# Layerscale on one core: the 4-row head of y loaded as one transfer or as two

## The chip, the core and the metric

The kernel runs on one core of a Trainium2 chip. The metric is device time in microseconds, the median over several runs. The core has a tensor engine (PE), a vector engine (DVE), a scalar engine (ACT), GpSimd (POOL) and a sync engine (SP). SP and ACT issue the transfers of this kernel; each has a queue of its own, and both queues are served by the same 16 transfer engines.

## The reference

```python
B, S, D = 1024, 16, 512          # x, y: bf16 [1024, 16, 512], gamma: bf16 [512]
def reference(x, y, gamma):
    return x + gamma * y
```

Flattened, x, y and the output are 16384 rows of 512 values, 1 KB a row and 16.8 MB a tensor.

## The kernel before

Each of the 128 partitions holds 128 rows. The tensors are cut into three blocks (BLOCKS) of 4, 64 and 60 rows per partition; within a block, partition p holds consecutive rows of memory, so a load of a whole block reads one run of 4, 64 or 60 KB for each partition, and each run is one packet. All of y stays in SBUF (y_sb) and is multiplied, added to and stored in place; x_sb is smaller and is used twice.

The order of all work is written out by hand in lists. SP lists the transfers of the sync engine, ACT those of the scalar engine: ('y', 0, 4) loads rows 0 to 3 of each partition's 128 rows of y, ('x', 4, 68, 4) loads rows 4 to 67 of x to x_sb from place 4 on, ('g',) loads gamma and ('s', 4, 68) stores rows. The function ring walks such a list and emits waits and transfers: L129 loads gamma, L132 x, L135 y, L138 stores. DVE lists the multiplications ('m', piece) and additions ('a', piece) over the five PIECES of 8, 16, 44, 52 and 8 rows; they are L180 and L189. Every wait goes through the helper _take (L35), which waits for a semaphore and sets it back.

Two constants shape the start. EARLY says how many entries of each list are moved to the very front of the program, ahead of its barriers (the loop at the end of the kernel function): two of SP's, one of ACT's. HOLD and AHEAD hold the rest back: before its entry number AHEAD, each of the two queues waits for one step of a semaphore (s_held) that TensorE gives when the load named HOLD has landed. TensorE itself then waits for gamma, spreads it over the partitions by a product with a row of ones (L152), and VectorE casts the result to gamma_sb (L154). VectorE takes a third step of s_held in place of waiting for the HOLD load. need(loads, c) emits the waits for the loads that a piece touches, in the order of the lists. The load named RELEASE, x rows 68 to 119, lets the stores begin (s_go).

So the start before is: SP issues y rows 0 to 3, then y rows 4 to 67; ACT issues x rows 0 to 3; when y rows 0 to 3 have landed, SP issues x rows 4 to 67 and y rows 68 to 127, and ACT issues gamma. The first multiplication covers rows 0 to 7 and thus needs y rows 4 to 67 too.

Of the kernel before, what the change touches and what calls it, by code (L numbers as in the profile page):

```python
# [9 lines left out]


SP = [
    ('y', 0, 4),
    ('y', 4, 68),
    ('x', 4, 68, 4),
    ('y', 68, 128),
# [2 lines left out]
]  # L19
ACT = [('x', 0, 4, 0), ('g',), ('s', 4, 68), ('s', 0, 4), ('s', 68, 128)]  # L20

EARLY = (2, 1)

HOLD, AHEAD = ('y', 0, 4), (2, 1)

RELEASE = ('x', 68, 120, 24)

# [10 lines left out]
def kernel(  # L38
# [74 lines left out]
    def ring(eng, what, n_early, n_ahead):  # L113

        known, went = 0, False
        for k, w in enumerate(what):
            kind = w[0]
            if k == n_ahead:
                _take(s_held[eng], 1, eng)
            need = frees(w) if kind == "x" else pieces_of(w[1], w[2]) + list(w[3:]) if kind == "s" else []  # L120
            need = max((order[c] + 1 for c in need), default=0)
            if kind == "s" and not went:
                _take(s_go, 1, eng)
                went = True
            if need > known:
                eng.wait_ge(s_add, need)
                known = need
            if kind == "g":
                i = eng.dma_start(out=gamma_row, in_=gamma.unsqueeze(0)).then_inc(s_gamma, 16)  # L129
            elif kind == "x":  # L130
                to = x_sb[:, w[3] : w[3] + w[2] - w[1], :]
                i = eng.dma_start(out=to, in_=rows_of(xf, w[1], w[2])).then_inc(s_load[w], 16)  # L132
            elif kind == "y":
                r = slice(w[1], w[2])
                i = eng.dma_start(out=y_sb[:, r, :], in_=rows_of(yf, w[1], w[2])).then_inc(s_load[w], 16)  # L135
            else:
                r = slice(w[1], w[2])
                i = eng.dma_start(out=rows_of(of, w[1], w[2]), in_=y_sb[:, r, :]).then_inc(s_out, 16)  # L138
            if k < n_early:
                early.append(i.ins)  # L140

    ring(nc.sync, SP, EARLY[0], AHEAD[0])
    ring(nc.scalar, ACT, EARLY[1], AHEAD[1])

# [89 lines left out]
```

## Time and profile before

| what | us |
|---|---|
| median of 3 runs (lowest, highest) | 119.66 (119.55, 119.72) |
| span of the profiled execution | 118.2 |
| its own time beyond the span | not recorded; the median is 1.5 longer than the span |
| VectorE busy | 70.1 |
| TensorE busy | 0.6 |
| bytes read, written | 33.56 MB, 16.78 MB |
| first issue by SP, by ACT | 0.00, 0.13 |
| first multiplication starts | 23.95 |
| last addition ends | 94.40 |

The span begins with SP's first transfer instruction and ends with its last wait. In the rows of the profile "DMA" is the busy share of the 16 transfer engines in 40 slices of the span, in tenths, and GB/s what they moved. A DMA issue row (SPq, ACTq) is the time that the issuing engine spent on the instruction, not the transfer. In the view of the DMA queues over a stretch, a packet counts where it starts, so a share can be over 100% when long packets start in a short stretch. The columns there are packets, MB and share of the 16 engines' time. A row of waits is: who waited, for whom, microseconds in total, how often, the longest.

### The profile page before, as it was taken

How to read it: one execution, taken by the hardware profiler on the slowest of the kernel's cores; microseconds unless marked ns; L12 is line 12 of the kernel's file. 1: busy time of each engine (PE TensorE's matmuls, PEld its weight loads, DVE VectorE, ACT ScalarE, POOL GpSimd, SP SyncE). 2: the span in 40 equal slices, each digit the busy share in tenths (PEclk: the TensorE clock that was granted, in tenths of full speed). 3: DMA queues.
4: the chain of work that ended last, by engine and by line, in shares of the span. 5: the costliest groups of instructions: out<-in, count | busy, mean ns of one | idle time of the engine just before them, and what ended most of it. 6: DMA issues, size and time to landing. Idle time of an engine off the chain costs nothing. (4 is left out here: it accounts for less than half of the span.)

```text
span 118.2 us, 91 instructions
## 1 busy us (share of the span) xinstructions
PE 0.6 (0%) x1; PEld 0.1 (0%) x1; DVE 70.1 (59%) x12; POOL 0.2 (0%) x4
## 2 busy tenths in 40 slices
PE   0000100000000000000000000000000000000000
PEld 0000000000000000000000000000000000000000
DVE  0000200089999969999999999999999900000000
POOL 0000000000000000000000000000000000000000
DMA  6999889988899879879969696898899889799793
GB/s 248 461 666 399 355 355 399 665 355 355 355 599 466 355 333 624 374 333 499 499 288 576 288 576 288 360 637 355 355 576 488 355 355 510 333 582 416 333 499 166
DMA packets 1442, 50.33 MB, mean 426 GB/s; under 512 B 161, under 2 KB 162, under 8 KB 546
## 3 DMA queue, kind: packets, MB, share of 16 engines
q1 hardware_dynamic: 864, 33.03, 64.8%
q10 hardware_dynamic: 578, 17.30, 33.9%
HBM read 33.56 MB, written 16.78 MB: 426 GB/s over the span
## 5 line engine op out<-in xcount | busy, mean ns | idle before, releaser
L180 DVE TENSOR_TENSOR y_sb<-y_sb,gamma_sb 128x4096 bf16<-128x4096 bf16 (+3 forms) x5 | 34.7, 6981 | 10.9 <-DVEq L35 10.9
L189 DVE TENSOR_TENSOR y_sb<-x_sb,y_sb 128x4096 bf16<-128x4096 bf16 (+3 forms) x5 | 34.7, 6981 | 1.2 <-DVEq L35 1.1
L154 DVE CAST gamma_sb<-gamma_ps 128x512 bf16<-128x512 f32 x1 | 0.7, 692 | 10.2 <-DVEq L35 10.2
L146 DVE MEMSET ones_row<- 1x128 bf16 x1 | 0.2, 165 | 2.0 <-PEq L51 2.0
L152 PE MATMUL gamma_ps<-gamma_row,ones_row 1*128 1x512 bf16 x1 | 0.6, 581 | 11.6 <-PEq L35 11.6
L152 PEld LDWEIGHTS gamma_ps<-gamma_row,ones_row 1*128 1x128 bf16 x1 | 0.1, 101 | 11.6 <-issue 11.6
L218 POOL MEMSET const-bfloat16-1.0<- 128x1 bf16 x1 | 0.1, 101 | 0.0
L218 POOL MEMSET const-uint8-127<- 128x1 uint8 x1 | 0.1, 101 | 0.0
L218 POOL MEMSET const-float32-0.0<- 128x1 f32 x1 | 0.1, 98 | 0.2 <-issue 0.2
L218 POOL MEMSET const-float32-1.0<- 128x1 f32 x1 | 0.1, 98 | 0.0
## 6 DMA issues: line engine op xcount, KB each, us to landing
y_sb<-in_y_dram SPq DMA_DIRECT2D x1, 7680.0 KB, 57.3
out_dram<-y_sb ACTq DMA_DIRECT2D x1, 7680.0 KB, 23.8
x_sb<-in_x_dram SPq DMA_DIRECT2D x1, 6656.0 KB, 21.7
x_sb<-in_x_dram SPq DMA_DIRECT2D x1, 1024.0 KB, 22.0
y_sb<-in_y_dram SPq DMA_DIRECT2D x1, 512.0 KB, 3.4
x_sb<-in_x_dram ACTq DMA_DIRECT2D x1, 512.0 KB, 4.2
out_dram<-y_sb ACTq DMA_DIRECT2D x1, 512.0 KB, 22.3
y_sb<-in_y_dram SPq DMA_DIRECT2D x1, 23.4
```

The source lines that it names most:

```text
L146: nc.vector.memset(ones_row, 1.0).then_inc(s_ones, 1)
L152: nc.tensor.matmul(gamma_ps, ones_row, gamma_row, start=True, stop=True).then_inc(s_ps, 1)
L154: nc.vector.tensor_copy(out=gamma_sb, in_=gamma_ps).then_inc(s_dve, 1)
L180: nc.vector.tensor_tensor(out=yt, in0=yt, in1=g, op=MULT).then_inc(s_dve, 1)
L189: nc.vector.tensor_tensor(out=yt, in0=xt, in1=yt, op=ADD).then_inc(s_add, 1)
L218: nc = _bacc.Bacc("TRN2", target_bir_lowering=False, num_devices=1)
```

## The change

The first entry of SP's list is replaced by two: rows 0 and 1, then rows 2 and 3. EARLY and AHEAD go from 2 to 3 for SP, so all three first entries stay at the front and ahead of the hold. HOLD names the first of the two, so SP's later entries, gamma and VectorE's step wait for rows 0 and 1; VectorE waits for rows 2 and 3 on their own semaphore. Nothing else differs: the same bytes go to the same places, and ACT's list, VectorE's list and the stores are as before. Within a partition the two halves are runs of 2 KB where the whole was one of 4 KB.

```diff
 SP = [
-    ('y', 0, 4),
+    ('y', 0, 2),
+    ('y', 2, 4),
     ('y', 4, 68),
     ('x', 4, 68, 4),
     ('y', 68, 128),
...
-EARLY = (2, 1)
-
-HOLD, AHEAD = ('y', 0, 4), (2, 1)
+EARLY = (3, 1)
+
+HOLD, AHEAD = ('y', 0, 2), (3, 1)
```

## The prediction

> **What bounds the kernel now.** I read the page first: the 40 slices and the DMA totals.
>
> ```profile
> span 118.2 us, 91 instructions
> DVE  0000200089999969999999999999999900000000
> ...
> DMA  6999889988899879879969696898899889799793
> ...
> DMA packets 1442, 50.33 MB, mean 426 GB/s; under 512 B 161, under 2 KB 162, under 8 KB 546
> ```
>
> VectorE (DVE) is idle in the first fifth and the last fifth, while the transfer engines are at 8 to 9 tenths in nearly every slice. Only the first slice starts empty: its 6 is one microsecond before the first packet. All 50.33 MB pass through 16 engines, and I find no stretch in which they wait for VectorE. So the end is set by two things: when the engines begin, and how long they stay fed.
>
> Next the waits of VectorE, to see what a delay would meet:
>
> ```profile
> DVE y_sb L180 <- DVEq L35: 10.9, 1, 10.9
> DVE gamma_sb L154 <- DVEq L35: 10.2, 1, 10.2
> ...
> DVE y_sb L189 <- DVEq L35: 1.1, 1, 1.1
> ```
>
> Its first multiplication (start 23.95) waits 10.9 us for y's rows 4 to 67 after the gamma cast (12.32 + 0.69); its first addition (43.45) waits 1.1 us for x's rows 4 to 67. VectorE follows the loads. Its last addition ends at 78.17 + 16.23 = 94.40, while the previous stores, on the same queue, still move packets until about 99.3. A delay of the head therefore reaches the end in full: no later hole in the DMA row can swallow it.
>
> Then the issues at the start, from the timeline:
>
> ```profile
> 0.00 0.85 SPq L135 DMA_DIRECT2D y_sb<-in_y_dram  x2
> 0.13 0.38 ACTq L132 DMA_DIRECT2D x_sb<-in_x_dram  x1
> ...
> 3.71 0.33 SPq L132 DMA_DIRECT2D x_sb<-in_x_dram  x1
> 3.90 0.50 ACTq L129 DMA_DIRECT2D gamma_row<-in_gamma_dram  x1
> 4.09 0.43 SPq L135 DMA_DIRECT2D y_sb<-in_y_dram  x1
> ```
>
> The three head loads (y 0 to 3 and y 4 to 67 by SP, x 0 to 3 by ACT) have all been issued by 0.85. When do their packets run? The DMA view of three stretches (0.90 to 2.20, 2.20 to 3.64, 3.64 to 4.00; packets count by their start; q1 is SP's queue, q10 ACT's):
>
> ```profile
> q1 hardware_dynamic: 102, 0.42, 84.8%
> ```
>
> ```profile
> DMA packets 163, 0.60 MB, mean 418 GB/s; under 512 B 16, under 2 KB 16, under 8 KB 163
> q10 hardware_dynamic: 121, 0.50, 85.2%
> q1 hardware_dynamic: 42, 0.11, 18.5%
> ```
>
> ```profile
> q1 hardware_dynamic: 16, 1.05, 689.3%
> q10 hardware_dynamic: 23, 0.03, 21.8%
> ```
>
> This is the heart of it. Until 2.20 there is not one packet of x, though x was issued at 0.13, only 0.13 after y's head, whose first packets run at 1.00. From about 2.2 the two queues alternate. The third load was issued at 0.42, yet until 3.64 no packet of 64 KB starts (all 163 are under 8 KB); then 16 start within 0.36 us, one on each engine. So the loads become ready for the engines one after the other, about 1.2 us apart, and not when they are issued. Now that costs nothing: a head load of 512 KB keeps the engines busy for 8 packets of 0.163 us each, 1.3 us, about as long as the next load takes to become ready.
>
> **The change part by part.**
>
> *Smaller packets.* Rows 0 to 3 are 128 runs of 4 KB; two loads make 256 runs of 2 KB, 16 per engine for 8. A 4 KB packet takes 1.04 x 16 engines x 1.44 us / 147 packets = 0.163 us (stretch 2.20 to 3.64, without the 16 completion writes). A 64 KB packet takes 62.7% x 16 x 4.60 / 19 = 2.43 us (stretch 4.00 to 8.60). The line through both is 0.038 us per KB plus 0.012 per packet. It gives 0.088 for 2 KB, so 8 x (2 x 0.088 - 0.163) = 0.10 us more per engine, with one more completion write 0.11. Bounds: not below 0, since the bytes are the same and the packets more; and 2 KB cannot cost more than two packets of 1 KB, of which gamma's takes 2.9% x 16 x 0.10 = 0.046, so at most 8 x (4 x 0.046 - 0.163) = 0.17, about 0.18 with the completion.
>
> *One more load in the row of loads.* Order of issue after: y 0-1 (SP, 0.00), x 0-3 (ACT, 0.13), y 2-3 (SP, 0.42), y 4-67 (SP, 0.85). Every load has 128 runs, as before. What does a load with 2 KB runs take to become ready? No row shows one. Nearest rows: y's head to x's, 2.21 - 1.00 = 1.21 us as upper end, and 1.05 as lower end, because an engine may have chosen one packet (0.16) ahead; x to y's 64 rows, at most 3.65 - 2.21 = 1.44. If the runs count, the half loads cost the same as the whole one. With 1.21 the four loads are ready at 1.00, 2.21, 3.42 and 4.63, and the 64 KB packets start at 4.63 where they started at 3.65: **+0.98 us**. With 1.05: 4.15, +0.50. With 1.21, 1.44, 1.44: 5.09, +1.44. On the engines: y 0-1 is gone after 8 x 0.088 = 0.7 us, by 1.7 to 2.1 (they start between 1.0 and 1.4), and they idle until x comes; x lasts 1.3 us, until 3.5 to 3.9; y 2-3 follows, done by 4.2 to 4.6, and they idle again until y 4-67. The 0.11 of the smaller packets lies inside this waiting and is not added. The other end is 0: were readiness proportional to bytes, the halves would cost half each, and only the 0.11 would be left. I take +0.98, since issue to first packet hardly follows bytes elsewhere: 1.00 us for 0.5 MB at the start, and 78.7 - 77.4 = 1.3 for a store of 8 MB.
>
> The Trainium skill speaks against this reading. "Perfetto Trace Analysis", section "DMA Instruction — HWDGE (DVE, Sync)", says that the profiled duration of a DMA instruction covers the making of all its descriptors and that the generator is free before that duration ends. By it the third load would be ready by 0.85 and the fourth by 1.27, and the change would cost the packets' 0.11 alone. The trace differs: x's issue ends at 0.51 and its first packet starts after 2.20, so I follow the rows and keep the page's answer as a rival.
>
> *SP's third issue ahead of the barrier.* 0.42 us (0.85 for two). The barrier behind it moves as much; ones_row's MEMSET at 1.99 becomes 2.41. TensorE waits for gamma until 11.56, so this is hidden; without that cover it would cost 0.42.
>
> *The hold.* It now waits for y 0-1. Before, the landing at 3.4 released SP's x load at 3.71. Landings come 0.35 after the last packet, so now about 2.1 + 0.35 = 2.5, and x 4-67, gamma and y 68-127 are issued some 0.9 us earlier. Worth nothing: on SP's queue they stand behind y 4-67, which runs to 23.8; gamma has 10.9 us of slack before L180. Queued behind the held instructions are only these.
>
> *VectorE's added wait* for y 2-3 stands ahead of its wait for y 4-67, which ends some 20 us later: 0.
>
> Sum on the profiled execution: span 118.2 + 0.98 = 119.2. The median of the runs shown, 119.66, has 1.5 us around that span; they stay: 119.66 + 0.98 = 120.64.
>
> **Rivals.**
> (1) *Readiness partly overlaps* (a step of 1.0): 64 KB packets at about 4.0, +0.35: 120.0. For it: one packet of choice ahead on each engine blurs the rows. Against: 16 of 16 engines turned to the third load only after 3.64.
> (2) *Not slower: only packets count.* Place: the engines' choice between queues after 2.2. If y 4-67 was ready early and an engine simply finished x's small packets before turning to 64 KB ones, no load is late and only +0.11 is left: 119.77. It decides if a step is under about 0.9 us, the time that 256 KB (0.7) and the engines' stagger cover. For it: no idle is seen at 3.65, a chance fit if loads are made at a rhythm of their own. Against: y's and x's packets do alternate after 2.2, and x's own lateness is not explained.
> (3) *Faster: the first load becomes ready sooner because it is half as big.* If the 0.63 us between the end of its issue (0.37) and its first packet (1.00) went by bytes, -0.31: 119.35. Against: the 8 MB store above.
> That SP blocks at its third issue would be a fourth; nothing due before 11.56 stands behind it, so it costs nothing by itself.
>
> **Chances.** +0.98 case 0.58; rival 1 0.12; rival 2 0.25; rival 3 0.05. The likeliest case's own range is 120.16 to 121.1; the range reaches down to 119.70 to take in rival 1 and half of rival 2. About 0.2% (0.24 us) is what a measurement can tell: faster is rival 3, 0.05; same is rival 2, 0.25; slower the rest, 0.70.
>
> **What would show it.** In the changed profile no x packet before about 2.2, low DMA share between 1.7 and 2.2 and again near 4.3 to 4.6, and the first 64 KB packets near 4.6; L180 starting at about 24.9. If the 64 KB packets start before 3.9, rival 2 is right. A changed length of the stretch after the head would make all of this wrong.

## The result, and the profile after

The changed kernel takes 120.21 us (median of 5, 120.12 to 120.26) beside 119.69 for the kernel before on the same chip: ratio 1.0043, 95% interval 1.0033 to 1.0054, so +0.52 us. It is slower, as forecast, by about half of the 0.98 that I expected. The profiled execution took 120.16 with a span of 118.8.

The page of the changed kernel:

```profile
span 118.8 us, 93 instructions
...
DMA  5999888998899879979969797898899889798791
...
DMA packets 1586, 50.33 MB, mean 424 GB/s; under 512 B 177, under 2 KB 178, under 8 KB 690
```

There are 144 packets more (128 by the split, 16 completion writes), and the first slice fell from 6 to 5. From the third slice on the row is nearly that of before. The loss is at the very start, and nothing gives it back later. VectorE's waits say the same:

```profile
DVE y_sb L181 <- DVEq L36: 11.3, 1, 11.3
DVE gamma_sb L155 <- DVEq L36: 10.0, 1, 10.0
...
DVE y_sb L190 <- DVEq L36: 1.0, 1, 1.0
```

The line numbers moved by one, the lengths of the waits by 0.4 or less. The first multiplication (L181) starts at 24.60 in place of 23.95, the first addition at 44.05 in place of 43.45: everything moved by about 0.6.

Where the 0.6 arises is read from three stretches of the start. The columns are the stretch, its length, the busy time of the compute engines, the clock, and last the DMA share and GB/s. First the kernel before, then the changed one:

```profile
1.00:2.20 1.20, 0.00 (x0) 0.00 (x0) 0.17 (x1) 0.00 (x0) 1.00 0.92 348
2.20:3.00 0.80, 0.00 (x0) 0.00 (x0) 0.00 (x0) 0.00 (x0) 1.00 1.06 420
3.00:3.40 0.40, 0.00 (x0) 0.00 (x0) 0.00 (x0) 0.00 (x0) 1.00 1.02 420
```

```profile
1.00:2.20 1.20, 0.00 (x0) 0.00 (x0) 0.00 (x0) 0.00 (x0) 1.00 0.80 222
2.20:3.00 0.80, 0.00 (x0) 0.00 (x0) 0.17 (x1) 0.00 (x0) 1.00 1.00 369
3.00:3.40 0.40, 0.00 (x0) 0.00 (x0) 0.00 (x0) 0.00 (x0) 1.00 0.96 389
```

The missing bytes are (348 - 222) x 1.2 + (420 - 369) x 0.8 + (420 - 389) x 0.4 = 151 + 41 + 12 = 204 KB. At 420 GB/s they are 0.49 us, close to the whole result, and three quarters of them are missing before 2.20. (Single traces of the same start differ by about 0.1 us here: the run held on rows 2 and 3 below, which starts like the changed kernel, has 176 GB/s in the first stretch, and the run with a late split, which starts like the kernel before, has 328.) The DMA view of that first stretch shows more, in the changed kernel and then in the kernel before:

```profile
DMA packets 128, 0.27 MB, mean 222 GB/s; under 512 B 7, under 2 KB 7, under 8 KB 128
q1 hardware_dynamic: 119, 0.23, 71.0%
q10 hardware_dynamic: 9, 0.04, 9.3%
```

```profile
DMA packets 102, 0.42 MB, mean 348 GB/s; under 512 B 0, under 2 KB 0, under 8 KB 102
q1 hardware_dynamic: 102, 0.42, 91.9%
```

SP's queue started 112 packets of 2 KB (119 less 7 completion writes) where it had started 102 of 4 KB: half the bytes at almost the same number of packets. At the 0.088 us a packet of the prediction the 16 engines had room for 16 x 1.2 / 0.088 = 218. Yet they were not simply empty: their busy share is 0.80 where it was 0.92, and SP's 71.0% are 71.0% x 16 x 1.2 / 112 = 0.12 us for each packet. The packets of rows 2 and 3, of the same size in the same kernel, take 87.5% x 16 x 0.36 / 60 = 0.084 between 3.64 and 4.00:

```profile
q1 hardware_dynamic: 60, 0.12, 87.5%
```

So part of the loss is emptier engines (0.12 x 1.2 = 0.14 us) and part is packets that last longer; these rows do not show why they do. And x (q10) has already begun: its first packet starts at 1.94 by the trace, while the last packet of rows 0 and 1 starts only at 2.61.

Last, the place at which I expected the second wait, 3.40 to 4.04 and 4.04 to 4.80 in the changed kernel:

```profile
q1 hardware_dynamic: 91, 0.19, 74.6%
q10 hardware_dynamic: 31, 0.07, 26.2%
```

```profile
DMA packets 70, 1.12 MB, mean 1480 GB/s; under 512 B 17, under 2 KB 17, under 8 KB 54
q1 hardware_dynamic: 69, 1.12, 344.9%
```

In the first the shares add up to 100%: rows 2 and 3 (q1) follow x's head (q10) without a hole. In the second, 16 packets of 64 KB start (70 less 54 under 8 KB). The trace has the first at 4.06 and the last at 4.72, where before they started from 3.65 to 3.99; the mean of the 16 is 4.27 for 3.79, 0.48 later. The predicted 4.63 for the first was too late, and the second hole did not come.

### The profile page after: what moved, and what is told of

Read it like the earlier page. It is cut to its first block, busy times and chain, and to the rows that moved or that the text cites. A ratio compares the mean times of both kernels' runs of the same rounds, so it can differ in the third digit from the quotient of the medians.

```text
span 118.8 us, 93 instructions
## 1 busy us (share of the span) xinstructions
PE 0.6 (0%) x1; PEld 0.1 (0%) x1; DVE 70.1 (59%) x12; POOL 0.2 (0%) x4
## 2 busy tenths in 40 slices
DMA packets 1586, 50.33 MB, mean 424 GB/s; under 512 B 177, under 2 KB 178, under 8 KB 690
## 5 line engine op out<-in xcount | busy, mean ns | idle before, releaser
L181 DVE TENSOR_TENSOR y_sb<-y_sb,gamma_sb 128x4096 bf16<-128x4096 bf16 (+3 forms) x5 | 34.6, 6981 | 11.3 <-DVEq L36 11.3
```

Of the source, the lines that this page charges most:

```text
L181: nc.vector.tensor_tensor(out=yt, in0=yt, in1=g, op=MULT).then_inc(s_dve, 1)
```

## The experiments

All times are medians beside the kernel before in the same session. Three theories were put to the test. S, the theory of the prediction: a load's packets become ready (so that an engine can run them) at about 1.0 to 1.2 us per 128 packets, whatever they hold, and short packets cannot cover that time. P: the same, but only the first load is paced so. C: the first 1.2 us of traffic are slow for any load. Beside them K: only the packets' own price counts.

**The short load in third place.**

```diff
 SP = [
     ('y', 0, 4),
-    ('y', 4, 68),
+    ('y', 4, 6),
+    ('y', 6, 68),
...
-EARLY = (2, 1)
+EARLY = (3, 1)
-HOLD, AHEAD = ('y', 0, 4), (2, 1)
+HOLD, AHEAD = ('y', 0, 4), (3, 1)
```

> The 2-row load is moved from first to third place: SP issues y 0 to 3, then y 4 and 5, then y 6 to 67; four loads at the start as in the changed kernel, and about as many packets. Theory P (paced first load: packets of the first load become ready at a fixed pace of about 0.14 us per packet and engine, so short packets waste the engines' time only there, while later loads are made ready behind it): only the packets' price, +0.1 us, about 119.8. Theory S (the recorded one: every load needs its own step of about 1.2 us before its packets can run): +0.5 to +1.0, 120.2 to 120.7. Theory C (the first 1.2 us of traffic are slow, whatever the load): +0.1, as P.

120.20 against 119.78, ratio 1.0033 (1.0021 to 1.0046): +0.4, just under S's range. P and C, which expected +0.1, do not account for it. The stretch 4.20 to 4.50 of this run holds almost only its 2 KB packets:

```profile
4.20:4.50 0.30, 0.00 (x0) 0.00 (x0) 0.00 (x0) 0.00 (x0) 1.00 1.03 328
```

328 GB/s in place of some 420, at a full busy share: these 2 KB packets take about 0.10 us each, not 0.084. The first packet of y 6 to 67 starts at 4.52, the last engine's at 5.25; before, the first 64 KB packets came from 3.65 to 3.99.

Not all of the trace's loss is made there. Its first stretch is slower than that of the kernel before (348 GB/s), though the first load is the same:

```profile
1.00:2.20 1.20, 0.00 (x0) 0.00 (x0) 0.00 (x0) 0.00 (x0) 1.00 0.93 297
```

With 394 for 420 in the next 0.8 us, that is 82 KB or 0.2 us. Whether the kernel or the single execution makes it is not shown.

**A longer load in third place.** The control to it: the third load has 8 rows, in 8 KB packets.

```diff
     ('y', 0, 4),
-    ('y', 4, 68),
+    ('y', 4, 12),
+    ('y', 12, 68),
...
-EARLY = (2, 1)
+EARLY = (3, 1)
-HOLD, AHEAD = ('y', 0, 4), (2, 1)
+HOLD, AHEAD = ('y', 0, 4), (3, 1)
```

> As the run with the short third load, but the third load has 8 rows (8 KB packets, 2.5 us of transfer) in place of 2 rows. S: the third load keeps the engines busy while the fourth is made ready, so the loss of the short third load goes: 0 to +0.1, 119.8 to 119.9. If an additional load at the start costs its step in any case: +0.4, as with the short one, 120.2.

119.81 against 119.72, ratio 1.0006 (0.9998 to 1.0015): nothing that can be told from no change. Its third load runs at nearly full rate until the fourth begins (6.20 by the trace):

```profile
3.80:5.00 1.20, 0.00 (x0) 0.00 (x0) 0.00 (x0) 0.00 (x0) 1.00 1.00 406
5.00:6.10 1.10, 0.00 (x0) 0.00 (x0) 0.00 (x0) 0.00 (x0) 1.00 1.03 424
```

The number of loads ahead of the long one, their place ahead of the barrier and the number of packets are those of the run above. Only the length of the third transfer differs (and with it the length of the fourth), and the 0.4 us goes. So this additional load costs nothing that can be measured, once it lasts long enough.

**The same split where the queue is full.** y's last block in place of its head:

```diff
-    ('y', 68, 128),
+    ('y', 68, 70),
+    ('y', 70, 128),
```

> The same kind of extra load, with 128 packets of 2 KB, is put where the queue is full: y 68 to 127 comes as y 68 and 69 and y 70 to 127, behind x 4 to 67, which keeps the engines busy for some 20 us before. S, in the form that 128 packets need about 1.0 to 1.2 us to become ready: there is time for that, so only the packets' price is left, 0 to +0.1, 119.8 to 119.9. K (the extra packets and the completion cost what the change cost): +0.4 to +0.5, as the changed kernel.

119.80 against 119.72, ratio 1.0005 (0.9996 to 1.0014). Its page counts the very packets of the changed kernel:

```profile
span 118.4 us, 93 instructions
...
DMA packets 1586, 50.33 MB, mean 425 GB/s; under 512 B 177, under 2 KB 178, under 8 KB 690
```

1586 packets, 690 of them under 8 KB, as in the changed kernel, yet without its loss. So the price of the packets and of the completion is at most 0.14% (the interval's end, 0.17 us), and K falls as the cause of the change's 0.52. The late split adds 8 packets per engine, as the change does. Rival 2 of the prediction, in which only the packets are left, falls with it.

**One load with twice the packets.** y's head is one load again, of 256 runs:

```diff
-                i = eng.dma_start(out=y_sb[:, r, :], in_=rows_of(yf, w[1], w[2])).then_inc(s_load[w], 16)
+                to, src = y_sb[:, r, :], rows_of(yf, w[1], w[2])
+                if w[1] == 0:
+                    to = to.rearrange("p (b n) d -> p b n d", b=2)
+                    src = yf[: 4 * P].rearrange("(b p n) d -> p b n d", b=2, p=P)
+                i = eng.dma_start(out=to, in_=src).then_inc(s_load[w], 16)
```

> y's head is one load of 512 KB again, but reads 256 runs of 2 KB in place of 128 of 4 KB (its 512 rows are taken in another order, so that y's head rows meet other rows of x: the output of those rows is another one). P with a pace per packet: the first load takes 16 packets x 0.14 = 2.2 us per engine in place of 1.3, so +0.8 to +0.9, 120.5. C: as the changed kernel, about +0.5, 120.2, since only the first 1.2 us are slow. S: three loads, no further step, +0.1, 119.8.

120.33 against 119.78, ratio 1.0041 (1.0028 to 1.0055). One load of 256 short packets costs what two loads of 128 cost. My reading of S as a step for each load (+0.1) missed, and P's +0.8 to +0.9 was too high; C's +0.5 came. Its stretch of 1.00 to 2.20:

```profile
1.00:2.20 1.20, 0.00 (x0) 0.00 (x0) 0.12 (x1) 0.00 (x0) 1.00 0.84 198
```

198 GB/s, like the changed kernel's 222, with y's head as a single load. So the loss does not need a second load; short packets in the first one are enough. One thing here speaks against loads that become ready strictly one after the other: x's first packet starts at 1.92 in this trace, long before the last of y's 256 (4.73), and the two queues alternate in between.

**A first load of one row.**

```diff
-    ('y', 0, 4),
+    ('y', 0, 1),
+    ('y', 1, 4),
...
-EARLY = (2, 1)
+EARLY = (3, 1)
-HOLD, AHEAD = ('y', 0, 4), (2, 1)
+HOLD, AHEAD = ('y', 0, 1), (3, 1)
```

> The head of y is split 1 and 3 rows in place of 2 and 2: the first load has 1 KB packets and 128 KB. P: the first load still takes about 1.1 us for 8 packets, but moves 128 KB less than the changed kernel's in it, 0.3 us of transfer that comes later: +0.3 against the changed kernel, +0.8 against before, 120.5. S: as the changed kernel, +0.5, 120.2. C, if the slowness is one of bytes per time: +0.5; if it is one of packets per time, as P.

120.60 against 119.78, ratio 1.0060 (1.0047 to 1.0073): +0.7 to +0.8. The expectation of a paced first load (P's +0.8, and C's if it counts packets) holds; S's +0.5, the unchanged loss, missed. The profiled execution took 120.25, the fastest of the five, so its trace shows less than the usual loss. Its DMA view of 1.00 to 2.20:

```profile
DMA packets 149, 0.18 MB, mean 146 GB/s; under 512 B 14, under 2 KB 137, under 8 KB 149
q1 hardware_dynamic: 137, 0.13, 45.0%
```

123 packets of 1 KB (137 less 14 completion writes) where it was 112 of 2 KB and 102 of 4 KB: nearly the same pace, 10 to 12 ns a packet over all engines, with 146, 222 and 348 GB/s. The 102 say the least, since at 0.163 us a packet the engines can run no more than 16 x 1.2 / 0.163 = 118.

**Rows 2 and 3 behind the long load.**

```diff
     ('y', 0, 2),
-    ('y', 2, 4),
     ('y', 4, 68),
+    ('y', 2, 4),
```

(beside the changed kernel).

> The changed kernel with its second and third SP loads exchanged: rows 0 and 1, then rows 4 to 67, then rows 2 and 3. S: the first gap (a first load of 256 KB that is gone before x's head is ready) stays, about 0.35 with the packets 0.45, so 120.15 to 120.25; the wait for a fourth load goes. If most of the change's loss is the fourth load's wait, this kernel is near before, 119.8 to 119.95.

120.38 against 119.72, ratio 1.0055 (1.0042 to 1.0067). No fourth load stands ahead of the long one here, and the loss is no smaller than the changed kernel's; it is a little above the 120.15 to 120.25 that S expected. So the change's loss is made at the first load of short packets, not by the wait for a fourth load. Its first stretch shows it, 189 GB/s:

```profile
1.00:2.20 1.20, 0.00 (x0) 0.00 (x0) 0.00 (x0) 0.00 (x0) 1.00 0.77 189
```

**The hold.** The changed kernel, held on rows 2 and 3:

```diff
-HOLD, AHEAD = ('y', 0, 2), (3, 1)
+HOLD, AHEAD = ('y', 2, 4), (3, 1)
```

> The changed kernel, but held on rows 2 and 3 in place of rows 0 and 1, so x 4 to 67, gamma and y 68 to 127 are issued about 2 us later. If the hold plays no part (as recorded): as the changed kernel, 120.2 to 120.3. If the earlier release adds traffic that slows the head: faster than the changed kernel by 0.1 or more.

120.25 against 119.80, ratio 1.0037 (1.0024 to 1.0050), within the interval of the changed kernel. x 4 to 67 is issued at 5.63 in place of 3.39, and it costs and gains nothing.

**Four loads of one row.**

```diff
-    ('y', 0, 4),
+    ('y', 0, 1),
+    ('y', 1, 2),
+    ('y', 2, 3),
+    ('y', 3, 4),
...
-EARLY = (2, 1)
+EARLY = (5, 1)
-HOLD, AHEAD = ('y', 0, 4), (2, 1)
+HOLD, AHEAD = ('y', 0, 1), (5, 1)
```

> y's head as four loads of one row, all at the front: six loads (with x's head) up to y 4 to 67. S: the sixth is ready at 1.0 + 5 steps of 1.0 to 1.17, 6.0 to 6.9 us, where the 64 KB packets of before start at 3.65: +2.3 to +3.2, 122.1 to 123. K: 8 more packets of 0.012 us per engine and load, about +0.3, 120.1.

121.27 against 119.80, ratio 1.0113 (1.0096 to 1.0130): +1.4, five times K's price, but about half of S's. The stretch 4.34 to 4.70 of this run:

```profile
DMA packets 119, 0.75 MB, mean 2085 GB/s; under 512 B 16, under 2 KB 109, under 8 KB 109
```

Ten packets of 64 KB (119 less 109) already start here, the first at 4.36 by the trace, after 640 packets; the last engine's comes at 5.72. That is (4.36 - 1.0) / 5 = 0.67 us per 128 packets for the first engine and, with the last engine's start taken as 1.4, (5.72 - 1.4) / 5 = 0.86 for the last. A fixed step of 1.0 to 1.2 is therefore wrong as a rule. The pace is not even through the run: the first 128 packets start from 1.01 to 2.38, and the other 384 of 1 KB all start from 3.31 to 4.98, 4 ns a packet in place of 11 (some of them may have been ready before).

**x's head as two loads.**

```diff
-ACT = [('x', 0, 4, 0), ('g',), ('s', 4, 68), ('s', 0, 4), ('s', 68, 128)]
+ACT = [('x', 0, 2, 0), ('x', 2, 4, 2), ('g',), ('s', 4, 68), ('s', 0, 4), ('s', 68, 128)]
-EARLY = (2, 1)
+EARLY = (2, 2)
-HOLD, AHEAD = ('y', 0, 4), (2, 1)
+HOLD, AHEAD = ('y', 0, 4), (2, 2)
```

> y's head stays one load; x's head, second in the row and on ACT's queue, comes as two loads of 2 rows, both ahead of the hold. P: the first load is whole and keeps the engines busy while x is made ready, so only the packets' price, +0.1 us, 119.8. S: one more step, +0.5 to +1.0. C: +0.1.

122.39 against 119.78, ratio 1.0216 (1.0202 to 1.0229): +2.6, which no theory expected. This run tells of something else. Its waits and, from the DMA issues, x's two head loads (median of both) and gamma:

```profile
DVE gamma_sb L154 <- DVEq L35: 27.4, 1, 27.4
...
DVE y_sb L180 <- DVEq L35: 0.4, 1, 0.4
```

```profile
x_sb<-in_x_dram ACTq DMA_DIRECT2D x2, 256.0 KB, 14.5
```

x's second load stands behind its first on ACT's queue, and now y 4 to 67 is ready before it. From then on the two queues alternate packet by packet: one of 2 KB, then one of 64 KB, so that 256 KB take some 20 us. From 6.00 to 24.00 either queue starts nearly the same number of packets, with 8.13 MB beside 0.25:

```profile
q1 hardware_dynamic: 137, 8.13, 104.1%
q10 hardware_dynamic: 135, 0.25, 3.6%
```

The Trainium skill, "DMA: Bandwidth & Descriptors", section "Queues, rings and completion order", says that each transfer engine goes round the queues that have work, packet by packet; this trace agrees. Gamma queues behind it, the cast waits 27.4 us, VectorE starts at 30.73 in place of 23.95 and frees x_sb so late that the second x load is issued at 61.23. The transfer engines starve between 60 and 64 (this run, then the kernel before):

```profile
q1 hardware_dynamic: 32, 0.85, 68.3%
```

```profile
q1 hardware_dynamic: 48, 1.70, 98.5%
```

Here 1.70 - 0.85 = 0.85 MB are missing, 2.0 us at the 426 GB/s of the kernel before. That leaves about 0.6 of the 2.6 for the start. By my estimate from the packets of both traces, with the bytes of a packet spread over its time, the run is 0.6 us behind at 5.0 us, of which 0.2 at 2.6 where both kernels still run the same y head. So the start alone lies nearer to S's +0.5 to +1.0 than to the +0.1 of P and C, but the time of this run, which mixes two effects, tests neither.

**The longest packets first.**

```diff
 SP = [
-    ('y', 0, 4),
     ('y', 4, 68),
+    ('y', 0, 4),
...
-ACT = [('x', 0, 4, 0), ('g',), ('s', 4, 68), ('s', 0, 4), ('s', 68, 128)]
+ACT = [('g',), ('x', 0, 4, 0), ('s', 4, 68), ('s', 0, 4), ('s', 68, 128)]
-EARLY = (2, 1)
+EARLY = (2, 2)
-HOLD, AHEAD = ('y', 0, 4), (2, 1)
+HOLD, AHEAD = ('y', 0, 4), (3, 2)
```

> SP issues y 4 to 67 (64 KB packets) first and y 0 to 3 second, both at the front; ACT issues gamma and then x 0 to 3 at the front; the hold is on y 0 to 3 and only y 68 to 127 and later loads stand behind it on SP. S (each 128 packets need about 1.0 to 1.2 us to become ready, whatever they hold): the engines are never without packets after the first 1.0 to 1.4 us, so the short first packets' loss goes, -0.1 to -0.2, 119.6, as long as VectorE, which now starts 1.3 us later, hides. K (only the price of packets counts): the number of packets is that of before, so 119.75, no difference.

120.22 against 119.80, ratio 1.0030 (1.0020 to 1.0040): slower by 0.4 where I expected a small gain. The first packets of the load, in 0.90 to 1.40 and then in 1.40 to 2.00:

```profile
q1 hardware_dynamic: 12, 0.79, 472.1%
```

```profile
DMA packets 4, 0.26 MB, mean 437 GB/s; under 512 B 0, under 2 KB 0, under 8 KB 0
```

Between 1.40 and 2.00 four engines start their very first packet. The first load's packets reach the 16 engines over 0.9 us (0.99 to 1.89 in the trace); in the kernel before all 16 were at work by 1.38. And the 12 that start earlier take 472.1% x 16 x 0.5 / 12 = 3.15 us each, where a 64 KB packet took 2.43 in the kernel before. Twelve packets that are 0.72 us too long are 0.54 us on the mean of 16 engines, so they alone could be the whole 0.4. Which of the two makes it, and why, no further run tests.

**Two loads cut by partitions.**

```diff
+                to, src = y_sb[:, r, :], rows_of(yf, w[1], w[2])
+                if w == HOLD:
+                    i = eng.dma_start(out=to[: P // 2], in_=src[: P // 2]).then_inc(s_load[w], 16)
+                    early.append(i.ins)
+                    to, src = to[P // 2 :], src[P // 2 :]
+                i = eng.dma_start(out=to, in_=src).then_inc(s_load[w], 16)
...
-    _take(s_load[HOLD], 16, nc.tensor)
+    _take(s_load[HOLD], 32, nc.tensor)
```

> y's head is two loads, as in the change, but cut by partitions: 64 runs of 4 KB each, 128 packets in all as before. If readiness goes by the packet: no more packets than before, so 119.8, +0.0 to +0.1. If each load has a step of its own of about 1.0 to 1.2 us: +0.4 to +0.6, as the changed kernel.

121.16 against 119.80, ratio 1.0118 (1.0093 to 1.0143): +1.4, beyond both. The view of 2.80 to 4.60 shows another effect:

```profile
q1 hardware_dynamic: 134, 0.48, 103.3%
```

103.3% x 16 x 1.8 us / 118 packets (134 less 16 completion writes) is 0.25 us for a 4 KB packet in place of 0.163. The order is another one too: x's packets run first, and y's first packet starts at 2.82. In 1.00 to 2.20 the queue of ACT is alone:

```profile
q10 hardware_dynamic: 62, 0.25, 80.3%
```

So the two loads of 64 partitions come later and run slower, and the run does not answer its question. Whether 64 partitions are the reason for the slower packets is not shown. The load of 256 runs answers the question from the other side.

## Why the prediction was right, and where its sizes were off

**Right: the bound and the path.** The transfer engines set the end. The loss of the start goes to the end unreduced: 0.49 us of missing bytes by 3.40, 0.6 at the first multiplication, 0.52 in the time. VectorE's waits keep their lengths within 0.4.

**Right in the main: the mechanism.** What runs at the start does not follow the bytes, and a head of short packets does not keep the 16 engines at their rate there. The load of 256 runs, the one-row first load (146 against 222 against 348 GB/s at nearly equal packets) and the pair of third loads (2 rows +0.4, 8 rows 0) show it. The late split, with the same 1586 packets, shows that they cost nothing where the queue is full.

**Wrong: where the engines lose.** I had rows 0 and 1 run at full rate, gone by 1.7 to 2.1, and the engines then empty until x at 2.21. By the trace the packets of rows 0 and 1 start over 1.6 us (0.99 to 2.61) and last 0.12 us each, and x begins at 1.94, before they are through. The first load is slow in itself, and behind it the busy share is 1.00 (2.20 to 3.00): no gap.

**Mis-sized: the step of 1.21 us for each load.** I put the four loads at 1.00, 2.21, 3.42 and 4.63. By the trace their first packets start at 0.99, 1.94, 3.42 and 4.06: steps of 0.95, 1.48 and 0.64. The third load came when I said. The fourth followed rows 2 and 3 on their own queue at once (8 packets per engine, 3.42 + 8 x 0.084 = 4.09), so it was ready by then and no step of it is left to see. I had carried one step over to all loads, and the run with four loads of one row shows that they are not alike.

**Too large by its own figures: the +0.98.** It is the shift of the earliest 64 KB packet, 3.65 to 4.63. But before, the 16 engines started theirs from 3.65 to 3.99, so for the mean engine (3.79) even 4.63 would be 0.84. And the empty times that I gave beside it, 0.1 to 0.5 and 0 to 0.4, come with the 0.11 of the packets to about 0.6. The measured mean shift is 0.48.

**Partly luck: the number.** Rival 1's step of 1.0 (+0.35) and the likeliest case (+0.98) have the measured +0.52 between them, and the low step of 1.05 gives +0.50. That agreement is no proof of a step of 1.05, because the measured steps are not equal and the loss lies at another place. Of the signs that I named, x not before 2.2 (1.94), 64 KB packets near 4.6 (4.06), a low share near 4.3 to 4.6 and the first multiplication at about 24.9 (24.60) did not come. The low share between 1.7 and 2.2 is there, but it begins at 1.00.

**Failed: the second idle time, near 4.3 to 4.6.** It did not come; rows 2 and 3 run into the 64 KB packets without a hole, and with these two exchanged the loss stays (+0.66, the intervals overlap). The whole loss is made before 3.40.

**Failed in size, and hidden: the hold.** I had x 4 to 67 issued at about 2.8; it was 3.39, since rows 0 and 1 landed 0.6 us later than full-rate packets would have. That it is worth nothing was right, as the run that is held on rows 2 and 3 shows.

**The rule that spoke against it.** The Trainium skill, "Perfetto Trace Analysis", section "DMA Instruction — HWDGE (DVE, Sync)", has all descriptors (the entries that tell a transfer engine what to move) made before the profiled duration of a DMA instruction ends. Here SP's first three issues end at 1.31, and the third load's first packet starts at 3.42. The +0.11 that I had worked out from the rule is not what was measured. The traces do not show the making of descriptors, so they do not say whether the rule fails or whether descriptors that are made still have to wait.

**Open.** What sets the pace, and why packets last longer at the start. With the same 384 packets ahead, the first long packet starts at 4.06 in the changed kernel (4.26 in the run held on rows 2 and 3, with the same start) and at 4.52 with the short load third; with 640 packets ahead it starts at 4.36. A fixed time per packet does not give all three. x's first packet starts at 2.21 to 2.40 in five traces with a first load of 4 KB packets and at 1.85 to 2.16 in six with shorter ones; an engine that is still on a 4 KB packet can explain 0.16 of that, and the rest is not explained. For the change taken alone, theory C counted in packets (the first 1.2 us are slow for any load) fits as well as S; what speaks against C is the short load in third place. Whether the making waits for earlier packets to be taken, or shares a path with the data, I did not separate.

## What to carry to other kernels

While nothing is queued yet, count a load by its packets, not by its bytes: here the first 1.2 us started 123 packets of 1 KB, 112 of 2 KB or 102 of 4 KB, so short packets there move few bytes. Of the first loads tried here the one of 4 KB packets was the best; 64 KB packets in first place lost 0.4 us as well. A load put in third place cost 0.4 us with 2 KB packets and nothing that can be measured with 8 KB packets. Once the queue is full, the same split costs nothing that can be measured. And a load whose first packet is read as "late" in a trace may only have stood behind other packets, as y 4 to 67 stood behind rows 2 and 3: such a time is an upper bound of its readiness, and one load's step need not be the next one's.

## What the runs showed of the hardware that I had not expected

- A small load on one queue beside a load of 64 KB packets on the other gets one packet in per round: 256 KB took some 20 us and made gamma's cast wait 27.4 us.
- The first packets of a start can last longer than later ones of the same size: 0.12 us for 0.084 at 2 KB in the changed kernel, 3.15 for 2.43 at 64 KB with the longest packets first.
- Two loads of 64 partitions ran at 0.25 us per 4 KB packet, those of 128 partitions at 0.163; and x's head, issued 0.12 us after the first of them, ran first (1.16 beside 2.82).
- With 64 KB packets first, the first packets of the 16 engines started over 0.9 us (0.99 to 1.89), and the kernel lost 0.4 us.
